# Reordered steps in the first stage of a one-core kernel: x copied out behind the logits, W's first step ahead of the state copy, raw W pieces loaded without a gate

## The chip, the core and the metric

The kernel runs on one core of a Trainium2 chip. A core has TensorE (PE, matrix products into PSUM; PEld is its weight load), VectorE (DVE), ScalarE (ACT), GpSimd (POOL) and SyncE (SP, which here only issues DMA transfers). Each engine works through its own list in order and waits on semaphores. TensorE runs at one of two clocks, 1.2 or 2.4 GHz, shown as the granted clock (0.5 or 1.0, or a mean of both). The metric is the device time of one execution in microseconds (us).

## The reference

Three parts in a row, all in float32:

```python
# 1: linear attention, batch 4, 8 heads, 768 steps, head size 48; a state per head
cur   = einsum(u * k_t, v_t);  y_t = r_t @ (state + cur)
state = w * state + outer(k_t, v_t)
# 2: x = y as 3072 tokens x 384; skip_score = x @ w_skip; tokens with score > 0:
logits = x @ w_gate;  e = argmax(logits);  g = softmax(logits)[e]
x += g * (relu(x @ w1[e]) @ w2[e])                 # 8 experts, 384 -> 1024 -> 384
# 3: out = (((x @ m1) * (x @ m2)) @ w3) @ w_out     # 384 -> 1024 -> 1024 -> 384
```

The matrices of part 3 are given in 64-bit floats.

## The kernel before, in words

The kernel folds w3 and w_out of part 3 into one matrix W = w3 @ w_out. It computes W while part 1 runs, as filler for TensorE. What the change touches is the loop of part 1 alone.

**The loop.** The 3072 tokens are 24 tiles of 128; tile n is a chunk of 64 steps for two batches (two tiles per chunk, each with its own state, hence the two names S and Ss with different numbers). The loop (line 813) runs n from 0 to 21, and the order in which it calls the helpers is the order on every engine. One pass n does, for tiles ahead and behind:

- DVE: `prep(n+2)` (FK, line 389, scales r and k; needs the load TB), on even chunks a scaling of the state (line 435), `evac(n+1)` (Fs, line 406, masks the scores sc), `bonus(n+1)` (lines 425 and 426, finishes Fs).
- ACT: `state_copy(n+1)` (Ss, line 437), `x_out(n)` (xg, line 468, copies y out of PSUM), xT (line 480), the logits' copy (line 494).
- PE: `scores(n+1)` (line 401), `y_mm(n)` (lines 447 and 450; needs Fs and Ss), then W products (`keep`, line 752; until W's parts are ready, dummy products of line 277), the logits of tile n-2 (line 491), the transposes of tile n-1 (line 478), W products again, `ds_mm(n)` (line 463, the state).
- SP: the store of xg to `xm` (two transfers), the load TB of tile n+4 (`load_t`), the load KV of tile n+4 (`load_v`).
- POOL: kd and m (lines 413 to 420).

The logits of tile n-2 are written into spare columns of the PSUM bank that holds y of tile n (or the bank G, which holds y of odd tiles). The accesses of one bank are kept in program order.

**W's work.** A generator (`w_steps`, line 662) turns 12 raw pieces of 64-bit words into the two parts (high and low) that the products use. A piece passes through: load (`raww`), ACT magnitude (line 111), ACT low bits (line 117), ACT signs (line 122), DVE join (`narrow`, line 140), ACT high part (line 688), DVE low part (line 695). There are two raw buffers, so after the join of piece i the load of piece i+2 may begin. Each `w_step(1)` does a third of a piece; `WN` says how many a pass takes, at three places: (1, 1, 1) for n from 2 to 6, and (1, 0, 1) from n = 7. Pieces 0, 2, 3 and 4 come from `in_wo` (768 KB), the others from `in_w` (1024 KB).

In the kernel before, `load_w` only notes that a piece is wanted. `load_wanted` issues one noted load a pass, and makes it wait for that pass's Fs (line 406).

Of the kernel before, what the change touches and what calls it, by code (L numbers as in the profile page):

```python
# [47 lines left out]
WK = [(1, 1)] * 9 + [(1, 2)] * 13  # L48
WN = [(0, 0, 0)] * 2 + [(1, 1, 1)] * 5 + [(1, 0, 1)] * 15
# [14 lines left out]
def fused_kernel(ctx, tc, att, kv, wt, u, wg, we, w3, wo, w12, r, k, v, wu, out):  # L64
# [14 lines left out]
    gate = con.tile([P, 2 * NE], F32, name="gate")  # L79
# [15 lines left out]
    def load_wide(pool, tag, src, ahead=2, gate=None):  # L95

        k = src.shape[1]
        if not wide:
            raw = pool.tile([P, k], F32, tag=tag, name=tag, bufs=ahead)
            dma = nc.sync.dma_start(out=raw, in_=src)  # L100
        else:
            raw = pool.tile([P, k, 2], I32, tag=tag, name=tag, bufs=ahead)
            dma = nc.sync.dma_start(out=raw.rearrange("p n w -> p (n w)"), in_=src.bitcast(I32))
        if gate:
            gate(dma)
        return raw
# [106 lines left out]
    def load_expert(e, q):  # L213
        raw = stg[(4 * e + q) % 3 // 2].tile([P, 2, 2 * D], F32, name="raw")
        nc.sync.dma_start(out=raw, in_=we[e, :, 2 * q:2 * q + 2, :])
        return raw
# [30 lines left out]
    with tc.manual_schedule():  # L247
# [13 lines left out]
        def load_v(n):  # L261
            c, bp = divmod(n, 2)
            nc.sync.dma_start(out=KV[bp][c % 2].rearrange("p a h d -> p (a h d)"), in_=kv[n])
# [11 lines left out]
        def dummy(n):  # L275
            bank = wp[1 - wf[0]] if spare[0] is None else spare[0]
            nc.tensor.matmul(bank[:, 0:n], zb[:, 0:P], zb[:, 0:n], start=True, stop=True)
# [17 lines left out]
                nc.gpsimd.affine_select(out=m, in_=m, compare_op=op, fill=fill, base=0,  # L295
                                        pattern=[[1, CH]], channel_multiplier=-1)
        jobs = [("o", 0), ("3", 0), ("o", 1), ("o", 2), ("o", 3)] + [("3", f) for f in range(1, NF)]
        raw_w, wanted = [], []

        def load_w(i):  # L300
            if i < len(jobs):
                wanted.append(i)

        def load_wanted(gate):

            if wanted:
                kind, q = jobs[wanted.pop(0)]
                raw_w.append(load_wide(nrp, "raww", wo[:, 2 * q * D:2 * q * D + 2 * D] if kind == "o" else w3[q], 2,
                                       lambda dma: behind(dma, gate, "transfers one after the other")))


        wc = ac.tile([P, 32], F32, name="wc")[:, 0:NH]
# [7 lines left out]
        for i in range(6):  # L320
            wn = pw[:, i - 1] if i else wc
            n = 1 << i
# [62 lines left out]
        def prep(n):  # L385

            t = TB[n % 3]
            FK = FK_[n] = wk.tile([P, 2, NH, CH], F32, name="FK", bufs=3)
            return nc.vector.tensor_tensor(out=FK, in0=t, in1=UT[:, n // 2 % 2], op=ALU.mult)

        def behind(later, earlier, reason="two operands from SBUF each"):

            tc.add_manual_dep(later.ins, earlier.ins.name, mybir.DependencyInfo(
                mybir.DependencyClass.Sync, mybir.DependencyReason.DATA), reason=reason)

        def scores(n):
            FK = FK_[n]
            sc = ps_1.tile([P, 512], F32, tag="sc", name="sc").rearrange("p (h t) -> p h t", h=NH)
            for h in range(NH):
                for m, d in zip(half, dims):  # L400
                    nc.tensor.matmul(sc[m, h], FK[d, 1, h], FK[d, 0, h], start=True, stop=True)  # L401
            return sc

        def evac(n, sc):
            Fs = Fs_[n] = wk.tile([P, NH, CH], F32, name="Fs")
            return nc.vector.tensor_tensor(out=Fs, in0=sc, in1=mask[:, None, :].to_broadcast([P, NH, CH]), op=ALU.mult)

        def prep_k(n):

            c, bp = divmod(n, 2)  # L410
            if c < NC - 1:
                kd = kd_[n] = wk.tile([P, NH, HD], F32, name="kd")
                return nc.gpsimd.tensor_tensor(out=kd, in0=KV[bp][c % 2][:, 1], in1=KU[:, c % 2], op=ALU.mult)
# [15 lines left out]
        def state_copy(n):  # L429
            c, bp = divmod(n, 2)  # L430
            s = S[bp]
            if c == 0:
                return
            if c % 2 == 0:
                nc.vector.tensor_tensor(out=s, in0=s, in1=w128[:, :, None].to_broadcast([P, NH, HD]),
                                        op=ALU.mult)
            nc.scalar.copy(out=Ss[bp], in_=s)

        def y_mm(n, tag="y"):

            c, bp = divmod(n, 2)
            v, Fs, FK = KV[bp][c % 2][:, 2], Fs_.pop(n), FK_.pop(n)
            y = G if n % 2 and n < NT - 2 else ps_1.tile([P, 512], F32, tag=tag, name="y")
            yv = y[:, 0:D].rearrange("p (h d) -> p h d", h=NH)
            for h in range(NH):
                for m in half:
                    nc.tensor.matmul(yv[m, h], Fs[m, h], v[m, h], start=(h == 0), stop=True, skip_group_check=True)
            for h in range(NH if c else 0):
                for m, d in zip(half, dims):
                    nc.tensor.matmul(yv[m, h], FK[d, 0, h], Ss[bp][d, h], start=False, stop=True,  # L450
                                     skip_group_check=True)
            y_[n] = y
            if n < NT - 2:
                yb[0] = y
# [10 lines left out]
        def x_out(n):  # L465
            c, bp = divmod(n, 2)
            xg = x_[n] = wk.tile([P, D], F32, name="xg", bufs=2)
            nc.scalar.copy(out=xg, in_=y_.pop(n)[:, 0:D])
            for q in range(2):
                r0 = (2 * bp + q) * NS + c * CH  # L470
                nc.sync.dma_start(out=xm[r0:r0 + CH, :], in_=xg[64 * q:64 * q + 64, :])
# [250 lines left out]
        def w_step(k):  # L722
            for _ in range(k):
                next(wprep, None)
# [10 lines left out]
        def w_ready():  # L735
            done.update(fresh[0])
            fresh[:] = fresh[1:] + [[]]
# [22 lines left out]
        def idle_mm():  # L760
            if spare[0] is None and w_out:
                w_evac(0)
            dummy(DQ)
            dummy(DQ)

        def keep(k):

            due[0] += k
            while due[0] > 0:
                if next(wmm, None):  # L770
                    due[0] -= 4
                else:
                    idle_mm()
                    due[0] -= 2
# [7 lines left out]
        sc = scores(0)  # L782
# [7 lines left out]
        nc.vector.tensor_tensor(out=w128, in0=pw[:, 5], in1=pw[:, 5], op=ALU.mult)  # L790
        bonus(0)
        more_consts = consts()
        load_w(0)
        load_v(2)
        load_v(3)
        nc.sync.dma_start(out=wgs, in_=wg)
        load_w(1)
        todo = []
        NEXT = {logits: logits_out, route_a: route_b, route_b: route_c}

        def run_todo(late=False):
            now, todo[:] = sorted(todo, key=lambda x: x[0] is not logits), []
            for fn, args in now:
                if late and fn is route_b:
                    todo.append((fn, args))
                    continue
                fn(*args)
                if fn is logits_out:
                    if args[0] in last_of:
                        todo.append((route_a, (last_of[args[0]],)))  # L810
                elif fn in NEXT:
                    todo.append((NEXT[fn], args))

        for n in range(NT - 2):
            w_ready()
            if n == NT - 3:
                raws = {q: load_expert(0, q) for q in range(2)}
            fk = prep(n + 2)
            state_copy(n + 1)
            sc = scores(n + 1)  # L820
            behind(prep_k(n + 1) or prep_m(n + 2), fk)
            if n < NT - 3:
                prep_m(n + 2)
            load_wanted(evac(n + 1, sc))
            bonus(n + 1)
            next(more_consts, None)
            w_step(WN[n][0])
            w_ready()
            if n == 0:
                for _ in range(NFIRST):  # L830
                    dummy(DQ)
            y_mm(n)
            x_out(n)
            if n + 4 < NT:
                load_t(n + 4)
            keep(4 * WK[n][0] if n else 0)
            run_todo()
            if n > 0:
                x_trans(n - 1)
            keep(4 * WK[n][1] if n else 0)  # L840
            w_step(WN[n][1])
            w_evac(0)
            ds_mm(n)
            place_mm(n % 2)
            if n + 4 < NT:
                load_v(n + 4)
            if n < NT - 3:
                place(3)
            w_step(WN[n][2])
            run_todo(n < NT - 3)  # L850
            if n > 0:
                todo.append((logits, (n - 1,)))
# [3 lines left out]
        sc = scores(b)  # L856
# [660 lines left out]
```

## Time and profile before

| | us |
|---|---|
| median of 3 runs | 653.38 (653.12 to 753.19) |
| the profiled execution | 653.81 |
| its span, first to last instruction | 652.0 |
| PE busy in the span | 617.2 (95%) |
| DVE, ACT, POOL busy | 453.8 (70%), 307.9 (47%), 137.4 (21%) |
| mean granted TensorE clock | 0.984 |

The profiled execution lies 0.4 us above the median, and its span is 1.8 us shorter than its own time. The busy shares are means over three parts with different limits: the loop of part 1 fills about the first 180 us, the experts go on to about 350 us, and the rest is part 3.

### The profile page before, as it was taken

To read this page: it belongs to the slowest core of one execution; us is meant where nothing else is said; L and a number is where in the kernel's file an instruction comes from. 1 tells how busy PE (TensorE), PEld (TensorE's weight loads), DVE (VectorE), ACT (ScalarE), POOL (GpSimd) and SP (SyncE) were. 2 spreads that over 40 slices of the span, in tenths; PEclk is the share of its full clock that TensorE was granted. 3 is DMA by queue.
4 is the path that set the end of the run, shared out by engine and by line. 5 is a ranking of instruction groups with operands and counts; after the bars stand their busy time and mean duration, and the time that the engine had idled before them with its cause. 6 is when DMAs were issued, how large, how long until landed. Compare 5 with 4: busy or idle time off the path is not lost.

```text
span 652.0 us, 15257 instructions
## 1 busy us (share of the span) xinstructions
PE 617.2 (95%) x6399; PEld 561.0 (86%) x6399; DVE 453.8 (70%) x807; ACT 307.9 (47%) x581; POOL 137.4 (21%) x143
## 2 busy tenths in 40 slices
PE   8788889999999999999998999999999999999996
PEld 7777778888988999899896988988988988988985
DVE  7757777586757789999985772772772772772770
ACT  1566866455226566666644533433433433433430
POOL 4934534343303122433222310000000000000000
PEclk9978989799999999999999999999999999999999
DMA  7978777575716877778722002002002002001001
GB/s 289 352 231 301 239 272 267 185 248 170 239 35 216 284 278 254 272 246 299 232 67 67 2 1 92 6 1 95 4 1 93 5 1 87 10 2 49 1 2 53
DMA packets 26940, 90.40 MB, mean 139 GB/s; under 512 B 4009, under 2 KB 10729, under 8 KB 25840
## 3 DMA queue, kind: packets, MB, share of 16 engines
q1 hardware_dynamic: 24816, 84.11, 38.0%
q0 software_dynamic: 2048, 5.24, 2.5%
q8 instruction: 52, 0.85, 0.5%
q14 instruction: 24, 0.20, 0.1%
HBM read 77.61 MB, written 12.39 MB: 138 GB/s over the span
## 4 chain that ended last, share of the span: by engine, by line
PE 65%; DVE 12%; issue 7%; DMA 7%; ACT 6%; POOL 2%; SPq 0%; POOLq 0%; ACTq 0%; DVEq 0%
PE po L1281 15%; PE xy L1240 10%; PE za L1240 10%; PE zb L1240 8%; PE hp L967 3%; PE wp L752 3%; DVE elo L91 3%; PE y L986 3%; PE S L463 2%; PE sc L401 2%; ACT raww L122 2%; DMA KV<-in_kv 2%; PE G L491 1%; DMA TB<-in_att 1%; DVE hl L971 1%
## 5 line engine op out<-in xcount | busy, mean ns | idle before, releaser
L1222 DVE TENSOR_TENSOR C<-st,za 128x512 f32<-128x512 f32 x47 | 32.3, 688 | 69.6 <-ACT st L1257 69.5
L91 DVE TENSOR_TENSOR elo<-raw,ehi 128x768 fp32r<-128x768 f32 x64 | 60.6, 952 | 3.7 <-ACT ehi L90 3.7
L1281 PE MATMUL po<-pl,W_hi 128*128 128x512 f32 (+1 forms) x152 | 58.2, 383 | 0.0
L1281 PE MATMUL po<-ph,W_hi 128*128 128x512 f32 (+1 forms) x152 | 58.1, 382 | 0.0
L1281 PE MATMUL po<-ph,W_lo 128*128 128x512 f32 (+1 forms) x152 | 57.6, 379 | 0.0
L967 PE MATMUL hp<-xh,ehi 128*128 128x240 f32 x192 | 54.5, 286 | 2.6 <-DVE hl L971 2.4
L1257 ACT COPY st<-xy 128x256 f32<-128x256 f32 x47 | 17.5, 372 | 81.8 <-PE xy L1240 81.8
L90 ACT CAST ehi<-raw 128x768 fp32r<-128x768 f32 x64 | 52.6, 829 | 1.5 <-DVE hl L971 1.5
L1240 PE MATMUL xy<-bxh,w12h 128*128 128x256 f32 x188 | 53.3, 284 | 0.0
L1240 PE MATMUL xy<-bxl,w12h 128*128 128x256 f32 x188 | 53.2, 283 | 0.0
L1240 PE MATMUL xy<-bxh,w12l 128*128 128x256 f32 x188 | 53.1, 283 | 0.0
L967 PE MATMUL hp<-xl,ehi 128*128 128x240 f32 x192 | 52.6, 276 | 0.0
L967 PE MATMUL hp<-xh,elo 128*128 128x240 f32 x192 | 52.4, 274 | 0.0
L1240 PE MATMUL za<-bxh,w12l 128*128 128x512 f32 x141 | 45.1, 320 | 0.0
L1240 PE MATMUL za<-bxh,w12h 128*128 128x512 f32 x141 | 45.0, 319 | 0.0
L1240 PE MATMUL za<-bxl,w12h 128*128 128x512 f32 x141 | 44.8, 318 | 0.0
L986 PE MATMUL y<-ehi,hh 128*128 128x384 f32 (+1 forms) x128 | 43.4, 339 | 0.0
L986 PE MATMUL y<-elo,hh 128*128 128x384 f32 (+1 forms) x128 | 43.2, 338 | 0.0
L986 PE MATMUL y<-ehi,hl 128*128 128x384 f32 (+1 forms) x128 | 43.2, 337 | 0.0
L967 PEld LDWEIGHTS hp<-xh,ehi 128*128 128x128 f32 x192 | 36.1, 189 | 7.2 <-DVE hl L971 6.8
L970 ACT ACTIVATE hh<-hp 128x240 fp32r<-128x240 f32 x64 | 23.6, 369 | 37.9 <-PE hp L967 35.1
L1005 POOL DMA_INDIRECT xm<-yo,sidx x16 | 23.3, 1457 | 83.9 <-DVE yo L1002 62.5
(260 smaller groups left out, 1773.3 us busy)
## 6 DMA issues: line engine op xcount, KB each, us to landing
raw<-in_we SPq DMA_DIRECT2D x32, 768.0 KB, 4.8
KV<-in_kv SPq DMA_DIRECT2D x24, 576.0 KB, 5.0
TB<-in_att SPq DMA_DIRECT2D x24, 512.0 KB, 6.1
raww<-in_w SPq DMA_DIRECT2D x8, 1024.0 KB, 6.4
raw<-in_w SPq DMA_DIRECT2D x8, 768.0 KB, 7.1
xm<-xg SPq DMA_DIRECT2D x48, 96.0 KB, 2.9
out<-ob SPq DMA_DIRECT2D x17, 256.0 KB, 2.0
x<-xm SPq DMA_DIRECT2D x20, 192.0 KB, 2.8
```

The costliest lines, as they stand in the source:

```text
L90: nc.scalar.copy(out=hi, in_=raw)
L91: (eng or nc.vector).tensor_tensor(out=lo, in0=raw, in1=hi.bitcast(F32), op=ALU.subtract)
L122: nc.scalar.activation(out=top, in_=raw[:, :, 1].bitcast(F32), func=AF.Copy, scale=2.0 ** -60)
L752: nc.tensor.matmul(ps, a[:, g], b[:, g], start=(g + i == 0), stop=(g == NF - 1 and i == 2))
L967: nc.tensor.matmul(hp, a, b, start=(i == 0), stop=(i == 8))
L970: nc.scalar.activation(out=hh, in_=hp, func=AF.Relu)
L986: nc.tensor.matmul(ys[e, t], a[:, P * t:P * t + ROWS[t]], b[:, D:2 * D], start=(f == 0 and i == 0), stop=(f == NF - 1 and i == 2))
L1005: ins = nc.gpsimd.indirect_dma_start(out=xm[:, :], out_offset=bass.IndirectOffsetOnAxis(ap=sidx[0:n, j, 1:2], axis=0), in_=yo, in_offset=N ...
L1222: nc.vector.tensor_tensor(out=halves(C[:, 0]), in0=st[:, 0:2], in1=halves(za), op=ALU.add)
L1240: nc.tensor.matmul(o, a, m, start=first and i == 0, stop=(i == 2), skip_group_check=True)
L1257: nc.scalar.copy(out=st[:, 0], in_=X)
L1281: nc.tensor.matmul(po, a[:, f, c], b[:, t], start=(i == 0), stop=(i == 3 * NF - 1))
```

## The change

Three edits in the loop of part 1.

1. `x_out(n)` and `load_t(n+4)` stand behind the W products and the logits (`run_todo`), no longer directly behind `y_mm(n)`.
2. The first `w_step` of a pass stands directly behind `prep(n+2)`, ahead of `state_copy`, `scores`, `evac` and `bonus`.
3. `load_w` issues the load at once where it is called, behind the join that frees the buffer. Only the first two loads, issued in the passes 0 and 1, wait for Fs as before.

```diff
-        raw_w, wanted = [], []
-
-        def load_w(i):
+        raw_w = []
+
+        def load_w(i, gate=None):
             if i < len(jobs):
-                wanted.append(i)
-
-        def load_wanted(gate):
-
-            if wanted:
-                kind, q = jobs[wanted.pop(0)]
+                kind, q = jobs[i]
                 raw_w.append(load_wide(nrp, "raww", wo[:, 2 * q * D:2 * q * D + 2 * D] if kind == "o" else w3[q], 2,
-                                       lambda dma: behind(dma, gate, "transfers one after the other")))
+                                       gate and (lambda dma: behind(dma, gate, "transfers one after the other"))))
...
-        load_w(0)
...
-        load_w(1)
...
             fk = prep(n + 2)
+            w_step(WN[n][0])
             state_copy(n + 1)
             sc = scores(n + 1)
             behind(prep_k(n + 1) or prep_m(n + 2), fk)
             if n < NT - 3:
                 prep_m(n + 2)
-            load_wanted(evac(n + 1, sc))
+            copied = evac(n + 1, sc)
+            if n < 2:
+                load_w(n, copied)
             bonus(n + 1)
             next(more_consts, None)
-            w_step(WN[n][0])
             w_ready()
...
             y_mm(n)
+            keep(4 * WK[n][0] if n else 0)
+            run_todo()
             x_out(n)
             if n + 4 < NT:
                 load_t(n + 4)
-            keep(4 * WK[n][0] if n else 0)
-            run_todo()
             if n > 0:
                 x_trans(n - 1)
```

The order on PE and on POOL stays as it was. The line numbers behind the edit fall by 5 (437 becomes 432, 468 becomes 463, 688 becomes 683, and so on).

On ACT, from the end of pass 9 to the copy of x in pass 12 (Ss is the state copy, xg the copy of x, L the logits' copy; raww, narw and W are a piece of W on its way, w3h its high part), before:

```order
L494 COPY L<-G 128x9
L437 COPY Ss_117<-S_204 128x384
L688 CAST w3h<-W 128x1024
L117 ACTIVATE raww<-raww 128x1024
L468 COPY xg<-y 128x384
...
L437 COPY Ss_116<-S_203 128x384
L111 ACTIVATE W<-raww 128x1024
L468 COPY xg<-G 128x384
...
L437 COPY Ss_117<-S_204 128x384
L122 ACTIVATE raww<-raww 128x1024
L468 COPY xg<-y 128x384
```

and with the change:

```order
L489 COPY L<-G 128x9
L683 CAST w3h<-W 128x1024
L117 ACTIVATE raww<-raww 128x1024
L432 COPY Ss_117<-S_204 128x384
L463 COPY xg<-y 128x384
...
L111 ACTIVATE W<-raww 128x1024
L432 COPY Ss_116<-S_203 128x384
L463 COPY xg<-G 128x384
...
L122 ACTIVATE raww<-raww 128x1024
L432 COPY Ss_117<-S_204 128x384
L463 COPY xg<-y 128x384
```

The state copy has moved behind the W work of its pass. The copy of x keeps its place on ACT in these passes; what it stands behind now is on PE (the logits that share its bank).

On DVE, pass 11 (FK is `prep`, Fs is `evac` and the end of `bonus`, narw is the join of a W piece), before:

```order
L389 TENSOR_TENSOR FK<-TB_119,UT 128x1024
L435 TENSOR_TENSOR S_203<-S_203,pw 128x384
L406 TENSOR_TENSOR Fs<-sc,mask 128x512
L425 TENSOR_REDUCE S_203<-m 128x8
L426 COPY_PREDICATED Fs<-diag,S_203 128x512
L140 SCALAR_TENSOR_TENSOR narw<-narw,raww 128x1024
```

and with the change:

```order
L384 TENSOR_TENSOR FK<-TB_119,UT 128x1024
L140 SCALAR_TENSOR_TENSOR narw<-narw,raww 128x1024
L430 TENSOR_TENSOR S_203<-S_203,pw 128x384
L401 TENSOR_TENSOR Fs<-sc,mask 128x512
L420 TENSOR_REDUCE S_203<-m 128x8
L421 COPY_PREDICATED Fs<-diag,S_203 128x512
```

In 8 of the passes a W step (the join of line 140 in 3, the low part of line 695 in 5) has moved ahead of the state's scaling, Fs and the bonus.

On SP, the passes 7 to 9 (raww is the load of a raw piece, xm the store of x, TB and KV the loads of tile n+4), before:

```order
L103 DMA raww<-in_w 128x2048
L471 DMA xm<-xg 64x384 x2
L259 DMA TB_120<-in_att 128x1024
L263 DMA KV_1_115<-in_kv 128x1152
L471 DMA xm<-xg 64x384 x2
L259 DMA TB_118<-in_att 128x1024
L263 DMA KV_0_112<-in_kv 128x1152
L103 DMA raww<-in_w 128x2048
L471 DMA xm<-xg 64x384 x2
```

and with the change:

```order
L103 DMA raww<-in_w 128x2048
L466 DMA xm<-xg 64x384 x2
L259 DMA TB_120<-in_att 128x1024
L263 DMA KV_1_115<-in_kv 128x1152
L103 DMA raww<-in_w 128x2048
L466 DMA xm<-xg 64x384 x2
L259 DMA TB_118<-in_att 128x1024
L263 DMA KV_0_112<-in_kv 128x1152
L466 DMA xm<-xg 64x384 x2
```

The second of these raw pieces stands one pass earlier. In the passes up to 7 the raw loads keep their place in SP's list and lose only the wait for Fs.

## Rows read from the trace of the kernel before

**Rows 1.** Waits of PE, 27.2 to 178.5 us: total us, times, longest.

```profile
PE G L491 <- ACT xg L468: 11.0, 6, 4.1
PE y L491 <- ACT xg L468: 7.4, 5, 2.0
```

**Rows 2.** Timeline of PE: start, duration, operation; in brackets the idle time before.

```profile
106.30 0.84 PE L491 MATMUL y<-wgs,xT 128*128 128x9 f32 x6 [0.25 <-ACT xg L468]
...
110.55 1.09 PE L447 MATMUL G<-KV,Fs 64*64 64x48 f32 x32
...
115.37 1.39 PE L491 MATMUL G<-wgs,xT 128*128 128x9 f32 x6 [2.08 <-ACT xg L468]
...
122.35 1.08 PE L447 MATMUL y<-KV,Fs 64*64 64x48 f32 x32
```

**Rows 3.** Timeline of PE: the starts of y of tiles 3, 8 and 22.

```profile
27.20 1.13 PE L447 MATMUL G<-KV,Fs 64*64 64x48 f32 x32
...
72.18 1.09 PE L447 MATMUL y<-KV,Fs 64*64 64x48 f32 x32
...
178.38 1.09 PE L447 MATMUL y<-KV,Fs 64*64 64x48 f32 x32
```

**Rows 4.** Windows, passes 3 to 7 and 8 to 21: stretch, us, busy times, PEclk, DMA share, GB/s.

```profile
27.20:72.20 45.00, 34.31 (x730) 30.91 (x728) 29.73 (x35) 29.22 (x41) 20.99 (x24) 0.89 0.80 275
72.20:178.40 106.20, 98.38 (x2084) 89.36 (x2081) 77.88 (x148) 57.54 (x95) 40.20 (x41) 0.95 0.71 230
```

**Rows 5.** Windows: the start of the loop, and the four slow stretches of PE.

```profile
16.00:28.00 12.00, 11.45 (x302) 10.32 (x297) 8.24 (x11) 6.10 (x9) 11.50 (x18) 1.00 0.96 339
33.80:40.00 6.20, 6.12 (x81) 5.52 (x81) 1.18 (x2) 3.63 (x5) 1.03 (x1) 0.50 0.74 247
60.50:64.50 4.00, 4.00 (x91) 3.97 (x92) 2.05 (x3) 1.92 (x2) 0.13 (x1) 0.57 0.97 350
91.00:95.00 4.00, 3.98 (x25) 3.54 (x27) 2.91 (x3) 2.23 (x2) 0.37 (x1) 0.57 0.91 317
115.40:122.40 7.00, 7.00 (x83) 6.56 (x83) 1.24 (x2) 4.36 (x5) 1.45 (x2) 0.51 0.45 139
```

**Rows 6.** Chain that ended last, 60 to 69 us: start, length, what.

```profile
60.60 1.82 ACT raww L122
...
62.45 0.04 DVE W L140
...
63.33 1.22 DVE FK L389
...
66.26 0.37 ACT Ss L437
66.63 0.73 ACT wo_h L688
67.37 1.03 ACT raww L117
68.40 0.36 ACT xg L468
```

**Rows 7.** Timeline of ACT and of DVE in pass 12.

```profile
103.40 2.52 ACT L122 ACTIVATE raww<-raww 128x1024 f16<-128x1024 f32 x1
...
104.71 0.74 DVE L426 COPY_PREDICATED Fs<-diag,S 128x512 f32<-128x512 int32 x1
```

**Rows 8.** Waits of ACT, DVE and SP's queue for W's pieces, 28 to 190 us.

```profile
ACT narw L111 <- DMA raww<-in_w: 5.6, 3, 2.8
...
DVE narw L140 <- ACT raww L122: 6.6, 2, 5.0
...
SPq L103 <- DVE Fs L406: 25.6, 10, 3.7
```

**Rows 9.** DMA view, 27.2 to 72.2 us: GB/s in 40 slices; packets and bytes.

```profile
GB/s 423 390 397 416 203 188 384 277 219 261 100 344 131 15 98 339 343 193 358 235 256 107 169 333 365 353 423 296 175 400 320 398 291 339 66 203 408 358 167 240
DMA packets 3401, 12.35 MB, mean 275 GB/s; under 512 B 465, under 2 KB 1241, under 8 KB 3136
```

## The prediction

> **What bounds the kernel now.** Everything that the change moves lies in the loop of part 1, so I read that stretch alone, and first of all what PE waits for there. The waits of PE [rows 1] have only two lines from 27.2 to 178.5 us: the logits of line 491 wait for ACT's copy of x, 11 times, 11.0 + 7.4 = 18.4 us. PE waits for nothing else in the loop. The data of the logits is not late: it is xT of two tiles before. What holds them is the bank. The copy of y (xg) is read from the bank into which the logits go, and it stands ahead of them in the program.
>
> A second cost follows from the first. In the timeline [rows 2] PE goes from the logits to the next y in 110.55 - 106.30 = 4.25 us after a wait of 0.25 us, and in 122.35 - 115.37 = 6.98 us after one of 2.08 us, with the same work between them. The windows say why [rows 5]: there are four stretches in which the granted clock is 0.50 to 0.57, that is mostly 1.2 GHz in place of 2.4. Each follows a longer wait at the logits. They last 6.2 + 4.0 + 4.0 + 7.0 = 21.2 us, and the pair of passes above prices them: 2.7 us lost in a stretch of 7.0, or 0.39 us lost for each us. That is 8.2 us in all, of which 4.0 in the first two stretches and 4.3 in the last two.
>
> Why is the copy of x late? The chain of waits [rows 6] shows it for pass 7: signs on ACT (60.60), join on DVE (62.45), FK (63.33), then the state copy on ACT (66.26), the high part (66.63), the low bits (67.37), and only then xg (68.40), on which PE waits. It is a ring through three engines: PE then does the logits and the transposes, ACT copies xT, and the next signs begin. No engine is full. In passes 3 to 7 PE is busy 34.3 of 45.0 us, DVE 29.7, ACT 29.2; in passes 8 to 21 they are busy 98.4, 77.9 and 57.5 of 106.2 us [rows 3, 4].
>
> **The change, part by part.** I make the sum against the profiled execution, 653.8 us, which is 0.4 above the median of the runs.
>
> *The copy of x behind the logits.* The logits no longer wait for xg; xg waits for them instead. On ACT that costs little: xg begins behind the logits' 0.84 us [rows 2] and the three W products ahead of them, but the instruction behind it, xT, needs the transposes that come after the logits anyway. So 18.4 us of wait lose their cause, and with them the 8.2 us of slow clock: at most 26.6 us, to 627.2. The stores of x and the load of TB move later with xg. From the logits of one pass to its next y are 4.25 us, which bounds the delay from above; TB is used two passes later, and a pass of PE's own work is 30.3 / 5 = 6.1 us (below), so that two passes cover it. Without that cover it would be the logits' 0.84 us a pass and more.
>
> *The first W step ahead of the state copy.* On ACT the state copy of tile n+1 now follows the high part and the low bits (0.73 + 1.03 us in rows 6), or the signs (2.52 us, rows 7). The bonus waits for the state copy and y of the next pass for the bonus. In pass 12 the bonus ended at 104.71 + 0.74 = 105.45 [rows 7], and the next y began at 110.55 [rows 2]: a margin of 5.1 us. A state copy later by 2.5 us stays inside it, so I cost it at nothing. On DVE, a join or a low part (0.88 us for a 768 KB piece, a third more for the others) ahead of Fs stays inside it too. What PE waits for next, where this is wrong, is y on Fs.
>
> It also gives something: the ring above gets shorter. What is left runs through ACT and the join alone: signs 1.82, join 63.33 - 62.45 = 0.88, high part 0.73, low bits 1.03, state copy 0.37, xg 0.36 and xT, which has xg's size, another 0.36: 5.6 us for a pass with a 768 KB piece [rows 6]. For one of 1024 KB the first four grow by a third, to an estimated 7.0.
>
> *The raw pieces without a gate.* SP waited 25.6 us in 10 waits for Fs before it could ask for a piece [rows 8]; 2.6 us each is what a load gains, and a whole pass for some pieces. ACT waited 5.6 us in 3 waits for the pieces of w3; these waits vanish as terms of their own, but they are causes of the late xg, so they are already inside the 18.4 us. In SP's queue nothing new is stuck behind the load's wait: the join stands on DVE ahead of all that xm and TB wait for.
>
> *What comes back.* In passes 3 to 7 the DMA engines set a floor. They move 12.35 MB there [rows 9]. In the start of the loop, with transfers always asked for, they kept 339 GB/s for 12 us at a busy share of 0.96 [rows 5]. At this rate 12.35 MB take 36.4 us; PE's own work is 34.3 - 4.0 = 30.3 us, and the ring above 5 x 5.6 = 28 to 5 x 7.0 = 35 us. I take 36.4 us, a gain of 45.0 - 36.4 = 8.6 us. Its bounds are 14.7 (PE alone) and 0 (the pieces still set the pace).
>
> In passes 8 to 21 the engines move 230 GB/s [rows 4], far below. PE's own work is 98.4 - 4.3 = 94.1 us. I leave one wait of 2.0 us, the size of the longest here [rows 2]: 96.1 us, a gain of 10.1 us, with bounds of 12.1 (no wait at all) and about 5 (half of it comes back as waits for Fs).
>
> What lies before 27.2 us and behind 178.4 us keeps its order but for pass 2, where magnitude and low bits of the first piece go ahead of the state copy: 0 to 1 us more, taken as 0. The later parts move up as a block.
>
> The sum: 653.8 - 8.6 - 10.1 = **635.1 us**. With the bounds of both stretches the forecast's own range is 629 to 642.
>
> **The rivals.**
>
> *The DMA engines are faster than I say.* Single slices of 1.1 us in passes 3 to 7 reach 423 GB/s [rows 9]; at 408 or more, PE's 30.3 us decide, and the time is 653.8 - 14.7 - 10.1 = 629 us. Against it: 339 is what a stretch of 12 us kept. The Trainium skill (DMA: Bandwidth & Descriptors, Bandwidth) gives about 425 GB/s for a transfer of 16 MB and 341 for one of 1 MB, measured with another kind of queue; by the first figure the stretch would take an estimated 29 us and the time would be this rival's, by the second it stays at mine. The row of 339 agrees with the second.
>
> *The pieces still set the pace in the first passes.* If a load asked for earlier only lands as late, because it shares the engines with TB and KV, ACT's magnitude waits as before and passes 3 to 7 stay at 45.0 us. For it: the share of 0.96 at the loop's start, and of 0.97 from 60.5 to 64.5 us, where an earlier request finds the engines full [rows 5]. Against it: the mean share of these passes is 0.80 [rows 4]. Only the later gain is left: 653.8 - 10.1 = 644 us.
>
> *The wait changes its name.* PE no longer waits at the logits but at y, for the bonus, since ACT is as late as before and now the state copy is what it delays. The margin of 5.1 us is then gained once and not in each pass: 649 to 653 us. Against it: ACT has work for 57.5 of 106.2 us and DVE for 77.9.
>
> *Slower: Fs behind a late W step.* In 8 passes DVE does a join or a low part ahead of Fs. Before, a join waited up to 5.0 us for the signs [rows 8], at a place where PE needed nothing from DVE. Now such a wait, and the 2.5 us of signs before the state copy, stand ahead of Fs and the bonus. It decides from the point where both together pass the margin of 5.1 us. If they did so by 5.0 + 2.5 - 5.1 = 2.4 us in each of 19 passes, this costs 46 us against the 26.6 that go: about 673 us. If only the 8 passes pay, it is 19 against 26.6 and no loss. It needs ACT to be late by a whole piece in every pass. The Trainium skill (TensorE: Matmul & The Clock Gate, the table at its head) calls the queues of ScalarE and VectorE strict FIFO, so that Fs could not pass a waiting join. The trace agrees: in the chain FK begins 0.88 us behind the join that had waited for ACT, and not before [rows 6].
>
> **How the numbers follow.** My forecast, 635 us, gets 0.64; the faster DMA (629) 0.08; the pieces' pace (644) 0.13; the changed name (651) 0.10; slower (673) 0.05. The range 628 to 646 takes in the first three and leaves out the last two and a little of the tails. Two per cent is 13 us, about what a measurement of this kernel can tell from no change, so faster means below 640.7: nearly all of the first two and a fifth of the third, 0.72. Within 2%: the rest of these and the changed name, 0.23. Slower: 0.05.
>
> **What would show it.** Right: the waits of line 486 (the old 491) for xg are gone; y of tile 8 begins near 63.6 us and y of tile 22 near 160; the granted clock of the loop is near 1.0; GB/s from 27 to 64 us is near 340. The pieces' pace would show as waits of ACT's line 111 for the load, with y of tile 8 still near 72. The changed name would show as waits of PE's y for DVE or for the state copy. I am wrong if PE finds a new wait longer than the margins above, or if the later parts do not move up with the loop.

## The result and the profile after

The changed kernel takes 633.21 us (median of 4 runs, 632.11 to 633.94) against 654.35 us of the kernel before in the same comparison: a ratio of 0.968, with a 95% interval of 0.965 to 0.971. One of the four runs of before took 753.19 us, a slow run that the ratio leaves out. The forecast was 635. The profiled execution took 633.43 us, with a span of 631.7 us and a mean granted clock of 0.989.

The busy line of its page, to be read beside the small table of before:

```profile
PE 609.8 (97%) x6399; PEld 558.6 (88%) x6399; DVE 455.6 (72%) x807; ACT 307.3 (49%) x581; POOL 141.4 (22%) x143
```

PE is busy for 7.4 us less with the same instructions (part of it ran at the slow clock before), and stands idle for less. Where that is, the waits of PE from 27 to 170 us tell (total us, times, longest):

```profile
PE y L442 <- ACT xT L475: 2.5, 2, 1.5
PE S L458 <- issue: 1.4, 1, 1.4
PE G L486 <- ACT xT L475: 0.6, 1, 0.6
```

Against [rows 1], the 18.4 us of waits of the logits for xg are gone. What is left is small and has other names. One of the names misleads. Before y of tile 6, DVE and PE did this:

```profile
48.56 0.56 DVE L420 TENSOR_REDUCE S<-m 128x8 f32<-128x384 f32 x1 [2.50 <-ACT Ss L432]
49.15 0.73 DVE L421 COPY_PREDICATED Fs<-diag,S 128x512 f32<-128x512 int32 x1
...
49.98 1.14 PE L442 MATMUL y<-KV,Fs 64*64 64x48 f32 x32 [1.52 <-ACT xT L475]
```

The copy xT ended at 49.22 us (48.84 + 0.38 in the chain below), the bonus at 49.15 + 0.73 = 49.88, and y began 0.10 us behind the bonus. Ahead of the other y that the list puts down to xT (0.95 us, at 78.22), and of two y whose short waits the profile names "issue" (0.2 us at 41.84, 0.3 at 92.50), the bonus ends 0.10 us before as well. So in these four passes PE waited 2.9 us in all for the bonus, and the bonus, at 48.56, for the state copy.

PE's timeline gives the starts of y that answer to [rows 3]:

```profile
29.68 1.73 PE L442 MATMUL G<-KV,Fs 64*64 64x48 f32 x32
...
64.77 1.09 PE L442 MATMUL y<-KV,Fs 64*64 64x48 f32 x32
...
157.99 1.09 PE L442 MATMUL y<-KV,Fs 64*64 64x48 f32 x32
```

So y of tile 3 begins at 29.68 us, y of tile 8 at 64.77, y of tile 22 at 157.99. Passes 3 to 7 take 35.1 us in place of 45.0, passes 8 to 21 take 93.2 in place of 106.2. From y of tile 22 to the end of the span it was 652.0 - 178.4 = 473.6 us, and is 631.7 - 158.0 = 473.7. The whole gain lies in the loop of part 1. The windows (busy us of PE, PEld, DVE, ACT and POOL, then the granted clock, the DMA share and GB/s) of the two stretches, and of two pieces of the first one:

```profile
29.70:64.80 35.10, 32.79 (x728) 30.62 (x726) 25.61 (x32) 27.60 (x38) 17.44 (x19) 0.88 0.89 312
64.80:158.00 93.20, 91.57 (x2084) 86.17 (x2079) 82.49 (x151) 57.32 (x95) 48.47 (x41) 1.00 0.77 264
...
45.00:50.00 5.00, 3.48 (x82) 3.12 (x79) 2.46 (x5) 4.42 (x8) 2.98 (x3) 1.00 0.91 351
50.00:60.00 10.00, 10.00 (x181) 9.47 (x183) 8.05 (x10) 7.04 (x10) 2.98 (x3) 0.66 0.94 318
```

In the long stretch PE is now busy for 91.6 of 93.2 us at full clock: it is the bound there. The short one is no such case. Of the four slow stretches of [rows 5] none is left at its place, but there is a new one from 50 to 60 us (clock 0.66), again behind idle time of PE (3.48 us busy of 5.00 before it). The chain of waits there, from the join of one raw piece to the join two pieces later, is this (start, length, what):

```profile
36.81 1.24 DVE narw L140
...
38.07 7.43 DMA raww<-in_wo
...
46.56 0.73 ACT wo_h L683
...
48.09 0.36 ACT Ss L432
...
48.84 0.38 ACT xT L475
49.22 1.82 ACT raww L122
...
51.06 0.97 DVE narw L140
```

The load is asked for right behind the join that frees its buffer. It lands 7.4 us later, and ACT takes it up at once. From join to join it is 51.06 - 36.81 = 14.25 us for two passes, 7.1 a pass: five of them make 35.6 us, and 35.1 were measured. The passes were not alike, though: 6.2, 5.9, 8.1, 9.0 and 5.8 us, the third with the wait at 49.98 us and gaps of 0.8, the fourth at the slow clock. So the sum alone does not show that this ring set the pace. The end of the stretch tells more: the bonus that y of tile 8 needs ended at 64.43 us, 0.34 us before y began. The chain to it has no step on PE from 49.22 us on, so with PE at full speed the stretch would have been shorter by 0.3 us at most. In [rows 6] the chain of pass 7 had no load in it; it ran through xg, on which PE waited.

The waits of ACT and of SP's queue for W's pieces, 15 to 175 us, which answer to [rows 8]:

```profile
ACT W L111 <- DMA raww<-in_w: 4.2, 2, 2.6
ACT narw L111 <- DMA raww<-in_w: 2.7, 2, 1.8
ACT narw L111 <- DMA raww<-in_wo: 2.7, 1, 2.7
...
SPq L103 <- DVE narw L140: 10.1, 5, 4.2
```

The 25.6 us in which SP's queue waited for Fs have become 10.1 us of waiting for the join. ACT still waits for pieces. The DMA view of 29.7 to 64.8 us answers to [rows 9] (packets and bytes; a queue that brings instructions; then KB of a transfer and the median us from issue to landing):

```profile
DMA packets 2873, 10.96 MB, mean 312 GB/s; under 512 B 380, under 2 KB 959, under 8 KB 2613
...
q8 instruction: 6, 0.10, 1.2%
...
raww<-in_w SPq DMA_DIRECT2D x2, 1024.0 KB, 7.4
raww<-in_wo SPq DMA_DIRECT2D x2, 768.0 KB, 7.3
```

The rate rose from 275 to 312 GB/s. In the kernel before, the same loads landed in 4.9 and 4.6 us in passes 3 to 7: asked for earlier, they now take longer to land.

### The profile page after: what moved, and what is told of

Same layout as the page of the kernel before. It is cut to its first block, busy times and chain, and to the rows that moved or that the text cites. A ratio compares the mean times of both kernels' runs of the same rounds, so it can differ in the third digit from the quotient of the medians.

```text
span 631.7 us, 15256 instructions
## 1 busy us (share of the span) xinstructions
PE 609.8 (97%) x6399; PEld 558.6 (88%) x6399; DVE 455.6 (72%) x807; ACT 307.3 (49%) x581; POOL 141.4 (22%) x143
## 4 chain that ended last, share of the span: by engine, by line
PE 71%; DVE 14%; DMA 6%; issue 4%; ACT 3%; POOL 1%; SPq 0%; DVEq 0%; ACTq 0%; POOLq 0%
PE po L1276 16%; PE xy L1235 11%; PE za L1235 10%; PE zb L1235 8%; PE hp L962 5%; PE y L981 4%; PE wp L747 3%; DVE elo L91 3%; PE sc L396 2%; PE S L458 2%; DVE hl L966 2%; DMA xr<-xm,sidx 1%; DMA raw<-in_w 1%; PE y L442 1%; DMA raww<-in_w 1%
## 5 line engine op out<-in xcount | busy, mean ns | idle before, releaser
L965 ACT ACTIVATE hh<-hp 128x240 fp32r<-128x240 f32 x64 | 23.7, 370 | 36.0 <-PE hp L962 35.9
L1000 POOL DMA_INDIRECT xm<-yo,sidx x16 | 21.8, 1359 | 84.7 <-DVE yo L997 53.8
```

The source lines that it names most:

```text
L965: nc.scalar.activation(out=hh, in_=hp, func=AF.Relu)
L1000: ins = nc.gpsimd.indirect_dma_start(out=xm[:, :], out_offset=bass.IndirectOffsetOnAxis(ap=sidx[0:n, j, 1:2], axis=0), in_=yo, in_offset=N ...
```

## The experiments

All times are medians; the ratio is to the kernel before, run on the same chip in turn (654.7, 653.2 and 654.9 us in the three groups of runs). Across the groups, gains are compared and not times.

### The three edits, one at a time and two at a time

| edits | us | ratio, 95% |
|---|---|---|
| 1 alone (x behind the logits) | 637.88 | 0.972, 0.967 to 0.977 |
| 2 alone (W step first) | 648.03 | 0.989, 0.986 to 0.992 |
| 3 alone (raw loads ungated) | 649.10 | 0.992, 0.989 to 0.996 |
| 2 and 3 | 648.55 | 0.990, 0.987 to 0.992 |
| 1 and 3 | 633.07 | 0.967, 0.962 to 0.972 |
| 1 and 2 | 634.56 | 0.970, 0.964 to 0.975 |
| all, run again | 631.69 | 0.966, 0.962 to 0.970 |

**Edit 1 alone**, in the kernel before:

```diff
             y_mm(n)
+            keep(4 * WK[n][0] if n else 0)
+            run_todo()
             x_out(n)
             if n + 4 < NT:
                 load_t(n + 4)
-            keep(4 * WK[n][0] if n else 0)
-            run_todo()
```

> Only the copy of x (with its stores and the load of TB) moves behind the logits; W's step and the gated raw loads stay as before. My theory: the cause of PE's 18.4 us of waits and of the slow clock is the order in the bank, so this edit alone takes most of it: no wait of the logits for xg, 638 to 644 us; the early passes keep the wait for gated pieces, y of tile 8 near 68 us. Rival (the raw pieces were late, and this is why ACT was late): ACT stays as late, PE waits at y instead, 648 us or more.

Measured 637.88 us, 16.8 less than before and just below the range. Its four runs lie in two pairs, 634.7 and 635.6, 640.2 and 640.6; the profiled execution is the longest, 640.64. Its largest wait of PE from 27 to 170 us, and ACT's for pieces of w3:

```profile
PE y L447 <- ACT wo_h L688: 1.9, 1, 1.9
...
ACT narw L111 <- DMA raww<-in_w: 5.2, 2, 4.0
```

No logits wait for xg. y of tile 8 begins at 64.44 us, not near 68: even with gated loads passes 3 to 7 took 64.44 - 27.88 = 36.6 us, nearly as in the full change. The time was lost one pass further on. y of tile 8 waits 1.9 us for the bonus (it ended at 64.34 us, 0.10 us before), and pass 8 then took 10.35 us, at a clock of 0.52 and with PE busy throughout. ACT's wait of 4.0 us comes only at 103 us, and PE does not wait there.

**Edit 2 alone**, in the kernel before:

```diff
             fk = prep(n + 2)
+            w_step(WN[n][0])
             state_copy(n + 1)
...
             next(more_consts, None)
-            w_step(WN[n][0])
```

> Only the first W step of a pass moves ahead of the state copy. My theory: xg keeps its place on ACT behind the same work, so the logits wait for it as before: 649 to 656 us, with 15 us or more of waits of the logits. Rival (the shorter ring through DVE and ACT is what counts): 640 to 646 us.

Measured 648.03 us, just below the range. In its profiled execution (656.78 us, the longest of the five, 8.8 above the median) the logits still wait for xg, 11.8 us in 6 waits and 2.1 in 4: 13.9 us of the 18.4.

**Edit 3 alone**, the changed kernel with the other two undone:

```diff
-            w_step(WN[n][0])
             state_copy(n + 1)
...
             next(more_consts, None)
+            w_step(WN[n][0])
...
-            keep(4 * WK[n][0] if n else 0)
-            run_todo()
             x_out(n)
             if n + 4 < NT:
                 load_t(n + 4)
+            keep(4 * WK[n][0] if n else 0)
+            run_todo()
```

> Only the raw pieces lose the wait for Fs; copy of x and W's step as before. My theory: the waits of ACT for pieces (6.5 us) shrink, the order in the bank still holds the logits: 645 to 650 us, with 10 us or more of waits of the logits left. Rival (late pieces are the root): 634 to 640 us, waits of the logits below 6 us.

Measured 649.10 us. The logits wait 9.0 + 5.2 = 14.2 us. Edits 2 and 3 each make xg somewhat earlier; neither takes its wait away.

**Edits 2 and 3**, the changed kernel with edit 1 undone:

```diff
             y_mm(n)
-            keep(4 * WK[n][0] if n else 0)
-            run_todo()
             x_out(n)
             if n + 4 < NT:
                 load_t(n + 4)
+            keep(4 * WK[n][0] if n else 0)
+            run_todo()
```

> The changed kernel with the copy of x put back directly behind y (W's step ahead and ungated pieces kept). My theory: the logits wait for xg again, 642 to 650 us. Rival (the other two edits do it): 632 to 637 us.

Measured 648.55 us: without edit 1 the kernel loses 15 of the 21 us. PE's waits, 27 to 180 us:

```profile
PE G L486 <- ACT xg L463: 5.8, 4, 2.9
PE y L486 <- ACT xg L463: 5.6, 6, 1.2
```

The wait of [rows 1] is there again, at 11.4 us. The two edits together are worth no more here than each by itself.

**Edits 1 and 3**, the changed kernel with edit 2 undone:

```diff
-            w_step(WN[n][0])
             state_copy(n + 1)
...
             next(more_consts, None)
+            w_step(WN[n][0])
```

> The changed kernel with W's first step put back behind the bonus (copy of x behind the logits and ungated pieces kept). My theory: ACT and DVE have margin in the late passes, and in the early ones the join comes at the end of a pass in both, so W's place matters little: 633 to 638 us. Rival (the shorter ring was what let PE run): 641 us or more, with new waits of y for Fs.

Measured 633.07 us; passes 3 to 7 take 61.94 - 27.27 = 34.7 us. The place of the W step makes no difference that these runs can tell once edits 1 and 3 are in.

**Edits 1 and 2**, with the gated loads of before (`load_wanted` as it was there; only the call is shown):

```diff
-                load_w(n, copied)
+            load_wanted(evac(n + 1, sc))
```

> The changed kernel with the gated raw loads of before (copy of x behind the logits and W's step ahead kept). My theory: pieces land late in a few passes, pass 8 above all, and PE waits there: 635 to 640 us. Rival (transfers one after the other are kinder to TB and KV, so that the gate is worth something): 630 to 633 us.

Measured 634.56 us, a hair below the expectation, with SP's raw loads waiting 31.3 us in 10 waits for Fs. Its interval and that of the full change overlap. So edit 1 carries 17 us. Beside it, edit 2 gains a further 1.8 us and edit 3 a further 3.3 by the medians, each against the kernel before in its own group, and both together 4 to 6; the intervals of all of these overlap, so the share of each is not shown.

### What bounds passes 3 to 7

**A third raw buffer.** If the DMA rate is a floor, this changes little; if the ring of a piece is, passes 3 to 7 get shorter. To make room it takes buffers from part 2 (xrp, s_oh), so only the loop can be compared.

```diff
-    xrp = xctx.enter_context(tc.tile_pool(name="xrp", bufs=6, side="right"))
+    xrp = xctx.enter_context(tc.tile_pool(name="xrp", bufs=4, side="right"))
...
-                raw_w.append(load_wide(..., 2,
+                raw_w.append(load_wide(..., 3,
...
-                    load_w(i + 2)
+                    load_w(i + 3)
...
-            if n < 2:
+            if n < 3:
                 load_w(n, copied)
```

> The changed kernel with three raw buffers in place of two (a piece may be asked for one piece earlier); to make room xrp has 4 buffers in place of 6 and s_oh 1 in place of 2, which can only slow later parts, so the early passes are read from the starts of y. Theory A (the DMA engines' rate is the floor of passes 3 to 7): y of tile 3 to y of tile 8 stays at 34 to 36 us. Theory B (the ring of a piece, load to join, is the floor since only two are on their way): 30 to 32.5 us.

Measured 669.09 us (1.026, 1.018 to 1.034). The loss lies behind the loop: y of tile 22 begins at 157.90 us, as in the changed kernel, and from there to the end it is 509 us in place of 474. Neither expectation of the loop held: passes 3 to 7 took 66.23 - 27.42 = 38.8 us, longer than in the changed kernel, though ACT did not wait for a piece once in them. The windows, and PE's timeline at the gaps:

```profile
27.40:40.00 12.60, 9.60 (x228) 8.89 (x223) 11.28 (x14) 9.18 (x13) 9.81 (x13) 0.95 1.02 410
40.00:66.20 26.20, 22.96 (x503) 21.08 (x504) 19.70 (x22) 20.40 (x29) 9.59 (x11) 0.89 0.88 290
```

```profile
36.02 0.39 PE L277 MATMUL wp<-zb 128*128 128x256 bf16 x2
38.62 0.42 PE L277 MATMUL wp<-zb 128*128 128x256 bf16 x2 [2.21 <-issue]
...
53.02 0.20 PE L442 MATMUL y<-KV,Fs 64*64 64x48 f32 x1 [1.23 <-issue]
```

Two things are to be seen. The DMA engines kept 410 GB/s for 12.6 us, so 339 GB/s is no limit. And PE stands still in the middle of a run of like products (between products 31 and 32 of y at 53 us, between two of the same two-product dummies at 36 us), where the profile names nothing that it waits for; with gaps of 0.79, 1.16 and 0.88 us that end at 32, 60 and 66 us that is 6.3 us. The third buffer did take the ring out of PE's way: y of the tiles 4 to 8 begins 1.6 to 5.3 us behind the bonus, and PE's 32.5 busy us and these gaps make up the whole 38.8.

**Fewer bytes.** The changed kernel without the KV loads of passes 3 to 7.

```diff
-            if n + 4 < NT:
+            if n + 4 < NT and not 3 <= n <= 7:
                 load_v(n + 4)
```

> The changed kernel without the loads KV that the passes 3 to 7 issue (the tiles 7 to 11 are computed with older data): 5 transfers, 2.9 MB of about 11 MB less in the early passes. Theory A (rate of the DMA engines): 8.1 MB at 339 GB/s are 24 us, so PE's own 30.3 us decide, y of tile 3 to y of tile 8 in 30 to 32 us. Theory B (ring of the piece): its load lands in 5 us in place of 7.5 and the ring gets shorter too, 30 to 33 us. Theory C (ACT's own work and the waits between ACT and DVE, not the transfers): 34 to 36 us as in the changed kernel.

Measured 632.40 us (628.97 to 637.70; the profiled execution was the slowest). Passes 3 to 7 took 34.2 us in it, which is theory C's range. The next version leaves out the loads of all passes up to 7:

```diff
-            if n + 4 < NT:
+            if n + 4 < NT and n > 7:
                 load_v(n + 4)
```

> The changed kernel without the loads KV that the passes 0 to 7 issue (the tiles 4 to 11 are computed with older data), so that the DMA engines are not full from 16 to 60 us. Theory A (full DMA engines are the floor of passes 3 to 7, and also hold back PE's supply of instructions, which the gaps without a named cause of about 2 us near 36 to 38 us show): these gaps go, y of tile 3 to y of tile 8 takes 30 to 32 us. Theory C (ACT and DVE are the floor, the gaps have another cause): 34 us or more, and the gaps stay.

Measured 630.25 us (0.963, 0.959 to 0.968). The window of passes 3 to 7, the first of PE's waits there, and the end of the chain that sets y of tile 8:

```profile
27.40:61.40 34.00, 29.65 (x727) 27.35 (x723) 28.24 (x33) 28.26 (x41) 19.40 (x23) 1.00 0.76 241
```

```profile
PE y L442 <- DVE Fs L421: 3.1, 2, 2.9
```

```profile
36.42 1.05 ACT w3h L683
...
39.97 1.83 DVE w3l L690
...
46.05 1.34 DVE wo_l L690
...
47.73 0.96 DVE narw L140
48.70 7.74 DMA raww<-in_w
...
56.53 0.47 ACT narw L111
...
57.73 0.73 ACT wo_h L683
58.47 1.03 ACT raww L117
59.49 0.37 ACT Ss L432
...
59.95 0.57 DVE S L420
...
60.55 0.74 DVE Fs L421
...
61.42 0.61 PE y L442 x14
```

With 241 GB/s in place of 312, the stretch is still 34.0 us long: the DMA rate is not its floor. What is, the timelines show: y of each of the tiles 4 to 8 begins 0.15 us behind the end of its bonus. From 29.3 to 48.7 us the chain goes to and fro between ACT and DVE (signs, join, high part, state copy, bonus, low part) and holds no load. Only the last raw piece is in it. This piece of 1024 KB takes 7.7 us to land here too and passes its lateness on: magnitude, high part, low bits, then the state copy behind them, the bonus, and y. That is theory C, except that the gaps of PE without a named cause are gone from 26 to 62 us. No run took work off ACT or DVE.

### Is the slow clock a price of its own?

The kernel before, with 80 dummy products in the four passes ahead of the slow stretches of [rows 5]. If the clock costs 8.2 us by itself, the kernel gets faster; if a ring through ACT, DVE and the loads sets the pace, it does not.

```diff
             keep(4 * WK[n][0] if n else 0)
+            for _ in range({3: 17, 6: 7, 10: 8, 13: 8}.get(n, 0)):
+                idle_mm()                     # two dummy products
             run_todo()
```

> The kernel before with filler products of zeros on PE ahead of the logits in the passes 3, 6, 10 and 13 (34, 14, 16 and 16 of them, about 0.11 us each), where PE waited 4.1, 1.7, 2.0 and 2.1 us and the clock then fell. They do no useful work. My theory (a wait costs twice, the second time by the clock): the four stretches at half clock go and with them up to 8 us, 645 to 649 us. Rival (the passes behind a wait are long for another reason): no gain, 653 to 657 us.

Measured 654.28 us (1.0005, 0.996 to 1.005). The window that held passes 3 to 7 before, one of the old slow stretches, and PE's waits from 27 to 185 us:

```profile
27.20:72.20 45.00, 37.32 (x731) 33.20 (x729) 29.12 (x34) 29.10 (x41) 20.22 (x22) 0.88 0.82 277
...
113.00:123.00 10.00, 9.01 (x190) 8.12 (x188) 4.96 (x7) 8.18 (x11) 3.22 (x4) 1.00 0.82 283
```

```profile
PE G L491 <- ACT xg L468: 6.0, 5, 3.3
PE y L491 <- ACT xg L468: 5.7, 3, 3.8
```

The clock is 1.00 from 113 to 123 us, where it had been 0.51 for 7 us, but the waits came in other passes (3.83 us at the logits at 43 us, one pass behind the first dummies) and the slow clock with them: the mean of the window is 0.88, beside 0.89 before. Passes 3 to 7 took 47.2 us here (74.18 - 27.01), and y of tile 22 began at 178.8 us, as before. So the slow clock was moved, not removed, and its price is not isolated. What the run does show: PE was busy 3.0 us more in this window than in [rows 4], and 3.7 us more in that of 72.2 to 178.4 us (102.05 us), at no cost in time. In the kernel before, PE's own speed was not what set the end of the loop.

### TB earlier, and the change once more

Edit 1 moves the load of TB back with xg. Here it goes to the head of the pass:

```diff
             fk = prep(n + 2)
+            if n + 4 < NT:
+                load_t(n + 4)
             w_step(WN[n][0])
...
             x_out(n)
-            if n + 4 < NT:
-                load_t(n + 4)
```

> The changed kernel with the load of TB put at the start of a pass (its buffer is free then), ahead of the stores of x in SP's list. In the changed kernel DVE waits 3 to 4 us for TB in passes 2 and 3. My theory: TB lands earlier in the first passes, 0 to 2 us better than the changed kernel. Rival: the DMA engines are full there, another transfer is late instead, no difference.

Measured 633.17 us (0.968, 0.964 to 0.971), beside 631.69 for the changed kernel in the same group: no gain. DVE waits for TB twice in the changed kernel up to 62 us, 3.4 us in all, and not at all here; nothing that PE needs hung on it. In this profile passes 3 to 7 took 38.8 us, of which 5.4 are gaps without a named cause. Of the versions that leave nothing out, none beat the changed kernel by more than the intervals.

The changed kernel again, with no edit:

> The changed kernel once more, on the chip and in the rounds of tb_early: 632 to 635 us.

Measured 631.69 us (629.73 to 636.00). Its windows of passes 3 to 7 and 8 to 21, and of pass 8 alone, first in the first profile and then in this one:

```profile
27.80:62.60 34.80, 30.02 (x728) 27.46 (x724) 27.03 (x33) 28.34 (x41) 19.58 (x23) 1.00 0.92 337
62.60:156.80 94.20, 94.17 (x2076) 88.96 (x2078) 82.86 (x151) 57.75 (x95) 48.55 (x41) 0.96 0.78 265
...
64.77:70.62 5.85, 5.85 (x149) 5.54 (x147) 5.72 (x10) 3.03 (x4) 3.83 (x3) 1.00 0.90 310
62.63:71.61 8.98, 8.98 (x143) 8.49 (x145) 8.61 (x15) 5.92 (x9) 4.58 (x4) 0.62 0.89 314
```

Beside the windows of the first profile they are an experiment that the chip made. In passes 3 to 7 the clock was 0.88 there and is 1.00 here, PE was busy 32.8 us and is 30.0, and the stretch takes 35.1 and 34.8 us: PE's clock does not set it. In passes 8 to 21 PE is never idle in this profile, and there the clock has a price. Pass 8 shows it best: PE is busy throughout in both profiles, for 5.85 us at a clock of 1.00 and for 8.98 at 0.62 (and for the 10.35 at 0.52 in the run of edit 1 alone). Over the whole of these passes 94.2 us at 0.96 stand beside 93.2 at 1.00, where PE had idled for 1.6.

## Why the prediction was right, and where it was not

| term | forecast | first profile | second profile |
|---|---|---|---|
| passes 3 to 7 | 36.4 us | 35.1 | 34.8 |
| passes 8 to 21 | 96.1 us | 93.2 | 94.2 |
| y of tile 3 later by | 0 to 1 us | 2.5 | 0.6 |
| behind y of tile 22 | as before | +0.1 | -0.1 |

Gain by the first profile: 9.9 + 13.0 - 2.5 - 0.1 = 20.3 us, which is the difference of the spans; 18.7 were forecast.

- **The wait for xg: right, and shown.** It is gone in every version with edit 1 and there in every one without it (13.9, 14.2, 11.4 and, with the dummy products, 11.7 us). Edit 1 alone gives 16.8 us, and taking it away costs 15.
- **Passes 8 to 21: the mechanism right, PE's work too large.** I took 94.1 us as PE's own work and left 2.0 us of wait. PE is busy 91.6 us at full clock and idle for 1.6. The mis-sized term is PE's work: I took 4.3 us off its 98.4 for the slow clock, and it fell by 6.8.
- **Passes 3 to 7: size right by luck, reason wrong.** The step that failed is "In passes 3 to 7 the DMA engines set a floor". I had taken the 339 GB/s of one stretch for what the engines can do. Later runs kept 398 GB/s (12 us of the changed kernel, run again) and 410 (three buffers), and with fewer bytes, at 241 GB/s, the stretch was as long. That the changed kernel came out at 312 and 337 GB/s, "near 340", is no proof of a floor. The Trainium skill (DMA: Bandwidth & Descriptors, Bandwidth) gives about 341 GB/s for 1 MB and 425 for 16 MB; I sided with the first figure, and the 410 measured with three buffers is nearer to the second.
- **What stands in its place** is the path through ACT and DVE to the bonus. y of tile 8, which ends the stretch, begins 0.10 to 0.34 us behind its bonus in both profiles of the changed kernel, with fewer KV loads (0.15 and 0.16), and in the runs of edit 1 alone, 1 and 2, and 1 and 3 (0.10 or 0.11). In the first profile of the change the path to it holds the load of a raw piece (7.4 us, with the ACT and DVE work on it 7.1 us a pass), as the rival on the pieces' pace said, but at 35 us and not at 45; with fewer bytes most of it holds ACT's and DVE's work alone, and it is as long. My ring of 5.6 to 7.0 us a pass left the load out and met its upper end, 35 us. Which of the two, load or work, would have to shrink is not shown: the run that took the ring out of PE's way (three buffers) got PE's gaps instead, 6.3 of its 38.8 us.
- **The slow clock.** Its price was right as a correction to PE's own work in passes 3 to 7 (30.3 us forecast, and PE is busy 30.0 at full clock), too small in 8 to 21. As a gain of its own it is at most 0.3 us in these passes of the first profile, where the bonus held y of tile 8; in passes 8 to 21, where PE is the bound, it is real (pass 8: 5.85 or 8.98 us). The sign that I had named, a granted clock near 1.0, held in passes 8 to 21 but not in 3 to 7 (0.88).
- **The W step costs nothing: right in the time, wrong on the margin.** With it at its old place the time is 633.1 us. But the step "a state copy later by 2.5 us stays inside it" failed: I had read the margin of 5.1 us from one pass, and in the changed kernel y waits for the bonus in four passes, 2.9 us in all, by the path that I had named (with fewer KV loads up to 2.9 us at once). So the rival of the changed name came true in part, with 2.9 of the 18.4 us. The gain that I gave to the step, a shorter ring, is nowhere clear of noise.
- **The raw pieces without a gate: partly right.** The gate's 25.6 us went, but the loads take 2.5 to 2.7 us longer to land, and ACT's waits stay. By the medians edit 3 is worth 3 us beside edit 1 and 2.5 to 4.6 beside edits 1 and 2, neither clear of noise.
- **Pass 2.** The 2.5 us of the first profile hold a gap of 1.37 us in PE without a named cause and the slow clock behind it; the second profile has 0.6. The new order alone does not bring them.
- **The slower rival** needed ACT late by a piece in each pass. ACT's waits for pieces came 8 times in the loop with at most 2.7 us.
- **The range.** The bounds that I gave for the two stretches add up to 627 to 649 us, and not to the 629 to 642 that I called the forecast's own range. The time lies inside both.

## What to carry to other kernels

When an engine waits for a copy out of a buffer that it only shares with that copy, look at the program's order first: putting the copy behind the small writer of the same bank was worth 16.8 us here, and two edits that merely made the copy earlier were worth some 6. When such a wait goes, look for the next ring with the loads in it, since a load that is asked for earlier may take longer to land (7.4 us here, 4.9 before). When a wait carries a name, check when the named work ended: here the bonus, and not the named copy, ended 0.10 us before PE went on. A rate that some stretch reached is a lower bound of what the DMA engines can do; before calling it a floor, take bytes away.

## What the runs showed of the hardware

**PE stands still at the same instructions, with no wait that the profile names.** In most runs with edit 1, PE has gaps marked "issue" in passes 3 to 7, up to 2.5 us long and most of them in the middle of a run of like products. Most come at the same places of the program: between products 3 and 4 of S in pass 3 (six runs), between two like dummy products in pass 4 (seven), between products 17 and 18 of y with Ss of tile 5 (three), ahead of the last of the 32 products of y of tile 6 (three). Left out are the short gaps so marked ahead of a y that begins 0.10 us behind its bonus. In us, for passes 3 to 7, where busy time, gaps and waits make up nearly the whole length:

| kernel | DMA share | PE busy | gaps | waits for DVE (Fs, bonus) | length |
|---|---|---|---|---|---|
| fewer KV loads (0 to 7) | 0.76 | 29.7 | 0 | 4.1 | 34.0 |
| fewer KV loads (3 to 7) | 0.79 | 30.6 | 1.6 | 2.0 | 34.2 |
| before | 0.80 | 34.3 | 0 | 0 (10.7 for xg) | 45.0 |
| TB earlier | 0.85 | 33.4 | 5.4 | 0 | 38.8 |
| changed, first profile | 0.89 | 32.8 | 0.6 | 1.7 | 35.1 |
| edits 2 and 3 | 0.89 | 34.4 | 0 | 0 (5.3 for xg) | 39.8 |
| edit 1 alone | 0.90 | 30.3 | 2.1 | 4.0 | 36.6 |
| edits 1 and 2 | 0.90 | 32.0 | 2.5 | 1.5 | 35.9 |
| edits 1 and 3 | 0.92 | 30.8 | 2.8 | 1.0 | 34.7 |
| changed, again | 0.92 | 30.0 | 2.6 | 2.2 | 34.8 |
| three raw buffers | 0.93 | 32.5 | 6.3 | 0 | 38.8 |

The mean share does not order them: 5.4 us at 0.85, 0.6 and 0 at 0.89. All the runs without edit 1, in which PE waits for xg, have none in these passes. The DMA view lists queues that bring instructions over the same engines (q8, 6 packets in 29.7 to 64.8 us). That PE waits for its own instructions would fit the fixed places, but no run shows it; the cause stays open.

**The same load takes longer with company, but not only with KV's.** In passes 3 to 7 a piece of 1024 KB landed in 4.9 us in the kernel before, in 7.4 in the changed one, and in 7.4 without the KV loads; one of 768 KB in 4.6, 7.3 and 5.2 us (medians of two or three loads). Why the large one did not get faster was not tried.
